# Half of batch 0's strided k moves to the software DMA queue, and every step stands in a new order

## The chip, the cores and the metric

The kernel runs on one core of a Trainium2 chip. TensorE (PE) does the matmuls, VectorE (DVE) and ScalarE (ACT) the elementwise work, GpSimd (POOL) issues most loads on a software DMA queue that converts float32 to bf16 on the way, and SyncE (SP) issues stores, transposing DMAs and plain loads on a hardware queue. The metric is device time in microseconds, lower is better; the median of the runs before is 285.81 us (three runs, 285.72 to 285.98).

## The reference

Sparse attention over 8 batches, 8 heads, 576 positions and 64 channels, followed by one dense two-layer network with the activation h·tanh(softplus(h)), which is Mish:

```python
rel = pos[:, None] - pos[None, :]
mask_local = (rel >= 0) & (rel < 32)
mask_strided = (rel >= 0) & (pos[None, :] % 32 == pos[:, None] % 32)
...
scores = np.where(masks, scale * (q @ k.T), -1e9)        # heads 0-3 local, heads 4-7 strided
attn_out = softmax(scores) @ v
x = attn_out.transpose(0, 2, 1, 3).reshape(4608, 512)
h = x @ w_in                                             # 512 -> 2048
out = (h * np.tanh(np.log1p(np.exp(h)))) @ w_out         # 2048 -> 512
```

## The kernel before

The 4608 tokens of the network are cut into nine blocks of 512 (block t is tokens 512t to 512t + 511). Both matrix products of a block are made with seven products in place of eight on 2x2 pieces, from prepared sums: `wis` and `wos` hold sums of pieces of the weights, `xs` sums of the tokens, `gs` sums of the activations. A block's first layer has four groups g of 512 hidden columns. Each group runs seven products of four 128x256 matmuls, on one of two PSUM sets: `set0` or `set1`, each one tile of two banks, with the single bank `ee0` or `ee1`. Between the products ACT copies one bank to the other, DVE adds a bank and a stored copy, and ACT takes three Mish activations into `gT`. Block 0 has its first 512 hidden columns made plainly (L684 is their Mish) and its second layer plainly too, while the sums of the weights are still being made.

Attention of batch b is worked in between. The strided heads are units of 72x72 scores, the local heads windows of 96 queries by 128 keys. q and k are transposed on PE for batches 0 to 2 (L201 strided, L207 local, copied out by ACT or DVE) and by transposing DMAs of SP for later ones. Scores go to the PSUM pair `at` or to banks of the sets, ACT takes exponentials into `Ps` and `Pl`, DVE masks them, PE multiplies by v (L306), DVE divides by the row sums (L318, L320) into `x_s` and `x_l`, and these are transposed into `xT`. `vs` is strided v spread with a column of ones from `vraw` (one step on DVE), and `vl` is local v with 32 rows copied between windows (the "share" step).

At the start nothing is in the chip. PE runs filler matmuls on `wis` (a memset tile) that nobody reads. SP's hardware queue loads batch 0's strided k as float32 into two halves, `hh[0]` and `hh[1]` (heads 4 and 5, heads 6 and 7); DVE and ACT cast one each into `ks`. POOL's software queue loads everything else.

The order is written out by hand-held strings of steps, one word each (such as `T:ks1:f@0`, the transposes of the second half of batch 0's ks into bank f). A program goes through the strings once, and every engine does its part of the words in that order and waits by semaphores where a tile is not ready. `D` and `A` at a word's end name DVE and ACT. A caret moves a word to the next block. Two words need to be known: `un` is a filler matmul, and `hold` makes POOL wait for a transposing DMA before it issues the loads behind it. Here is the part of the start that speaks of k:

```python
for hp in range(2):
    stage_ks(hp)
...
"ld:qs@0 ld:vs@0 kc:0:D kc:1:A un:1:a un:1:a ..."
```

Of the kernel before, what the change touches and what calls it, by code (L numbers as in the profile page):

```python
# [19 lines left out]
SU = 80  # L20
# [25 lines left out]
def kernel(ctx, tc, q, k, v, moe_w_in, moe_w_out, out):  # L46
# [81 lines left out]
    def load_str(b, n, src):  # L128
        if b == 0:
            Po.dma_start(raw[n][0:SU], rows80(src, 4, 4))  # L130
        else:
            Po.dma_start(raw[n][0:PN], src[b, 4:8].rearrange("h (p j) d -> p h (j d)", j=CS))

    def stage_ks(hp):
        nc.sync.dma_start(hh[hp][0:SU], rows80(k, 4 + 2 * hp, 2))

    def cast_ks(hp, eng):
        cast(eng, ks[0:SU, 2 * hp:2 * hp + 2, :], hh[hp][0:SU])
# [32 lines left out]
    def load_w_in(f0, f1):  # L171
        Po.dma_start(w_in[:, :, f0:f1], moe_w_in.rearrange("(cc p) f -> p cc f", p=128)[:, :, f0:f1])
# [382 lines left out]
    with tc.manual_schedule():  # L555
        Sc.preload_act_table(AF.Exp)
        Sc.dma_start(consts[:], consts_h.ap())
        for hp in range(2):
            stage_ks(hp)
# [48 lines left out]
        def do(w, t):  # L608
            if w[0] == "^":
                w, t = w[1:], t + 1  # L610
# [16 lines left out]
            elif f == "kc":  # L627
                cast_ks(int(x[0]), eng)
            elif f == "wi":
                load_w_in(int(x[0]), int(x[1]))  # L630
# [84 lines left out]
        def go(plan, t=0):  # L715
# [3 lines left out]
        IN = (  # L719
# [23 lines left out]
        )  # L743
        SECOND = (
# [7 lines left out]
        )  # L752
# [99 lines left out]
```

## Time and profile before

| what | value |
|---|---|
| median of three runs | 285.81 us |
| the profiled execution | 286.13 us |
| its span, first to last instruction | 284.4 us |
| PE busy | 276.1 us, 97% |
| DVE, ACT busy | 220.4 us, 193.1 us |
| granted TensorE clock | 1.00 |
| software queue, hardware queue moved | 18.62 MB, 19.14 MB |

The profile is of one execution. Busy time of PE counts a matmul from its start to its modelled end, so back-to-back matmuls overlap in it, and short waits between matmuls can stand inside busy time. The bracket behind a row of the trace is the time in which the engine was idle just before, and what ended it. A DMA's landing time runs from its issue to the moment at which a waiting engine sees it.

### The profile page before, as it was taken

How to read it: one execution, taken by the hardware profiler on the slowest of the kernel's cores; microseconds unless marked ns; L12 is line 12 of the kernel's file. 1: busy time of each engine (PE TensorE's matmuls, PEld its weight loads, DVE VectorE, ACT ScalarE, POOL GpSimd, SP SyncE). 2: the span in 40 equal slices, each digit the busy share in tenths (PEclk: the TensorE clock that was granted, in tenths of full speed). 3: DMA queues.
4: the chain of work that ended last, by engine and by line, in shares of the span. 5: the costliest groups of instructions: out<-in, count | busy, mean ns of one | idle time of the engine just before them, and what ended most of it. 6: DMA issues, size and time to landing. Idle time of an engine off the chain costs nothing.

```text
span 284.4 us, 7635 instructions
## 1 busy us (share of the span) xinstructions
PE 276.1 (97%) x3242; PEld 226.4 (80%) x3242; DVE 220.4 (77%) x376; ACT 193.1 (68%) x296; POOL 51.8 (18%) x65
## 2 busy tenths in 40 slices
PE   8889999999999999999999999999999999999994
PEld 2656845668988888988898888898888888888883
DVE  2588978899897897999798969885999656835753
ACT  2686884599867777669765986678879427525830
POOL 8423321350007005200350044002000000000000
PEclk9999999999999999999999999999999999999999
DMA  7999999999849988999799979998472030003003
GB/s 157 191 206 204 205 189 199 103 222 167 148 90 93 131 154 150 205 145 170 208 143 126 179 204 160 121 168 189 97 190 48 2 120 28 2 3 148 2 0 148
DMA packets 103826, 38.50 MB, mean 135 GB/s; under 512 B 85384, under 2 KB 99112, under 8 KB 103792
## 3 DMA queue, kind: packets, MB, share of 16 engines
q0 software_dynamic: 61296, 18.62, 66.7%
q1 hardware_dynamic: 42208, 19.14, 28.3%
q8 instruction: 25, 0.41, 0.6%
q10 hardware_dynamic: 288, 0.25, 0.4%
q14 instruction: 9, 0.07, 0.1%
HBM read 38.03 MB, written 9.44 MB: 167 GB/s over the span
## 4 chain that ended last, share of the span: by engine, by line
PE 90%; DMA 3%; ACT 3%; DVE 1%; issue 1%; POOL 0%; ACTq 0%; DVEq 0%; POOLq 0%
PE set L121 57%; PE ee L121 21%; PE at L306 5%; PE at L121 4%; DMA kl<-in_k_dram 3%; PE at L350 1%; PE ee L207 1%; PE ee L350 1%; ACT osb L110 1%; DVE ee L115 1%; PE set L306 0%; ACT kTl L110 0%; ACT gT L684 0%; ACT Ps L273 0%; DVE x_s L320 0%
## 5 line engine op out<-in xcount | busy, mean ns | idle before, releaser
L121 PEld LDWEIGHTS <-wis 128*128 128x128 bf16 x578 | 55.7, 98 | 11.6 <-issue 2.9
L121 PEld LDWEIGHTS <-gs 128*128 128x128 bf16 x512 | 48.9, 98 | 6.3
L121 PEld LDWEIGHTS <-gT 128*128 128x128 bf16 x448 | 42.1, 98 | 9.4
L121 PEld LDWEIGHTS <-w_in 128*128 128x128 bf16 x436 | 41.1, 97 | 8.1 <-issue 1.0
L121 PE MATMUL set<-xT,w_in 128*128 128x256 bf16 (+1 forms) x296 | 45.8, 278 | 0.4 <-ACT gT L684 0.2
L121 PE MATMUL set<-w_out,gT 128*128 128x256 bf16 (+1 forms) x304 | 46.2, 295 | 0.0
L448 ACT ACTIVATE gT<-set 128x1024 bf16<-128x1024 f32 x35 | 35.9, 1025 | 12.6 <-PE set L121 12.3
L121 PE MATMUL set<-xs,wis 128*128 128x256 bf16 x280 | 42.0, 272 | 0.3 <-DVE ee L115 0.2
L110 ACT COPY set<-set 128x512 f32<-128x512 f32 x37 | 21.4, 577 | 18.8 <-PE set L121 18.3
L115 DVE TENSOR_TENSOR hh<-set,hh 128x512 f32<-128x512 f32 x35 | 24.0, 686 | 7.2 <-PE set L121 6.9
L115 DVE TENSOR_TENSOR ee<-set,hh 128x512 f32<-128x512 f32 x35 | 24.4, 697 | 5.7 <-PE set L121 4.0
L121 PE MATMUL set<-wos,gs 128*128 128x256 bf16 x224 | 27.8, 273 | 0.0
L446 ACT ACTIVATE gT<-hh 128x512 bf16<-128x512 f32 x35 | 21.7, 633 | 1.8 <-DVE hh L115 1.6
L115 DVE TENSOR_TENSOR gs<-gT,gs 128x2048 bf16<-128x2048 bf16 x16 | 19.5, 1219 | 3.3 <-issue 1.0
L673 POOL COPY hold<-xT 1x2 bf16<-1x2 bf16 x6 | 2.3, 381 | 105.4 <-DMA xT<-x_l 105.4
L444 ACT ACTIVATE gT<-ee 128x512 bf16<-128x512 f32 x35 | 20.0, 596 | 2.0 <-PE ee L121 2.0
L121 PE MATMUL ee<-xs,wis 128*128 128x256 bf16 x140 | 21.0, 273 | 0.0
L121 PE MATMUL set<-xs,w_in 128*128 128x256 bf16 x140 | 21.0, 272 | 0.0
L121 PE MATMUL ee<-xT,wis 128*128 128x256 bf16 x140 | 21.0, 273 | 0.0
L115 DVE TENSOR_TENSOR gs<-gT 128x2048 bf16<-128x2048 bf16 x16 | 19.5, 1217 | 0.0
L320 DVE TENSOR_TENSOR x_s<-at,rden 72x768 bf16<-72x768 f32 (+1 forms) x22 | 18.8, 856 | 0.8
L121 PE MATMUL ee<-wos,gT 128*128 128x256 bf16 x128 | 16.1, 273 | 0.0
(135 smaller groups left out, 439.7 us busy)
## 6 DMA issues: line engine op xcount, KB each, us to landing
out_dram<-osb SPq DMA_DIRECT2D x17, 512.0 KB, 3.3
ql<-in_q_dram POOLq DMA_DIRECT2D x8, 288.0 KB, 11.9
vl<-in_v_dram POOLq DMA_DIRECT2D x8, 288.0 KB, 12.0
w_in<-in_moe_w_in_dram POOLq DMA_DIRECT2D x4, 512.0 KB, 15.0
w_out<-in_moe_w_out_dram POOLq DMA_DIRECT2D x4, 512.0 KB, 16.9
ks<-in_k_dram POOLq DMA_DIRECT2D x7, 288.0 KB, 11.2
qs<-in_q_dram POOLq DMA_DIRECT2D x7, 288.0 KB, 10.4
vraw<-in_v_dram POOLq DMA_DIRECT2D x7, 288.0 KB, 9.4
```

The costliest lines, as they stand in the source:

```text
L110: Sc.copy(out_, in_)
L115: eng.tensor_tensor(out=out_, in0=a, in1=b, op=op)
L121: PE.matmul(o, lhsT=lhsT, rhs=rhs, start=start, stop=stop, skip_group_check=True)
L207: PE.transpose(tr[64 * e:64 * e + 64, PL * j:PL * j + PL], src[0:PL, 2 * hp + e, j, :], ident[0:PL, 0:PL],)
L306: PE.matmul(po[:, (n - n0) // per, (n - n0) % per, :], lhsT=pt[0:r, c0:c0 + 128], rhs=rhs, start=True, stop=True,)
L320: Dv.tensor_tensor(out=xo, in0=po[0:m, :, :, 0:D], in1=rd.unsqueeze(3).to_broadcast([m, nb, per, D]), op=ALU.mult,)
L350: PE.transpose(tr[:, n * j:n * j + n], x[0:n, u:u + 2, :].rearrange("p u d -> p (u d)"), ident[0:n, 0:n],)
L444: Sc.activation(o[:, 0:2, 256:512], two(E), AF.Mish)
L446: Sc.activation(o[:, 2:4, 256:512], two(h[:, 1, :]), AF.Mish)
L448: Sc.activation(o[:, :, 0:256].rearrange("p (b u) n -> p b u n", b=2), SET[z][:, 0:2, :].rearrange("p b (u n) -> p b u n", u=2), AF.Mish,)
L673: Po.tensor_copy(hold[0:1, 0:2], src)
```

## The change

Of batch 0's strided k, SP loads and ACT casts only the first half (heads 4 and 5); the software queue loads the second half straight into `ks`, as its first load. The `w_in` loads can take part of the rows, and a leading underscore moves a word one block back. All strings are replaced by a list with one string for each of ten stages, so that no two blocks share one, and the order of the words is new throughout: the order was made by counting a two-bank PSUM tile as one thing that is busy or free, where a bank was counted before.

```diff
     def load_str(b, n, src):
         if b == 0:
-            Po.dma_start(raw[n][0:SU], rows80(src, 4, 4))
+            h = 2 if n == "ks" else 0
+            Po.dma_start(raw[n][0:SU, h:4], rows80(src, 4 + h, 4 - h))
...
-    def stage_ks(hp):
-        nc.sync.dma_start(hh[hp][0:SU], rows80(k, 4 + 2 * hp, 2))
-
-    def cast_ks(hp, eng):
-        cast(eng, ks[0:SU, 2 * hp:2 * hp + 2, :], hh[hp][0:SU])
+    def stage_ks():
+        nc.sync.dma_start(hh[0][0:SU], rows80(k, 4, 2))
+
+    def cast_ks(eng):
+        cast(eng, ks[0:SU, 0:2, :], hh[0][0:SU])
...
-    def load_w_in(f0, f1):
-        Po.dma_start(w_in[:, :, f0:f1], moe_w_in.rearrange("(cc p) f -> p cc f", p=128)[:, :, f0:f1])
+    def load_w_in(f0, f1, c0=0, c1=4):
+        Po.dma_start(w_in[:, c0:c1, f0:f1], moe_w_in.rearrange("(cc p) f -> p cc f", p=128)[:, c0:c1, f0:f1])
...
-        for hp in range(2):
-            stage_ks(hp)
+        stage_ks()
...
-            if w[0] == "^":
-                w, t = w[1:], t + 1
+            while w[0] in "^_":
+                w, t = w[1:], t + (1 if w[0] == "^" else -1)
...
-            "ld:qs@0 ld:vs@0 kc:0:D kc:1:A un:1:a un:1:a un:1:a un:1:a un:1:a un:1:a un:1:a un:1:a clear:1 clear:0 b:s1:C@0 "
+                "ld:ks@0 un:1:a un:1:a ld:qs@0 un:1:a un:1:a un:1:a un:1:a un:1:a un:1:a ld:kl@0 kc:A clear:1 un:1:a "
...
-        go(IN)
-        go(SECOND, 1)
...
+        for t, plan in enumerate(PLANS):
+            go(plan, t)
```

Three places show what moves. The first is POOL at the start, which issues the loads of the software queue. Before:

```order
L130 DMA qs<-in_q_dram 80x4x512
L154 DMA vraw<-in_v_dram 80x4x512
L143 DMA kl<-in_k_dram 96x4x384
L143 DMA ql<-in_q_dram 96x4x384
L159 DMA vl_78<-in_v_dram 96x24x64
L172 DMA w_in<-in_moe_w_in_dram 128x4x512 x3
L132 DMA ks<-in_k_dram 72x4x512
```

And now:

```order
L131 DMA ks<-in_k_dram 80x2x512
L131 DMA qs<-in_q_dram 80x4x512
L144 DMA kl<-in_k_dram 96x4x384
L155 DMA vraw<-in_v_dram 80x4x512
L144 DMA ql<-in_q_dram 96x4x384
L160 DMA vl_78<-in_v_dram 96x24x64
L173 DMA w_in<-in_moe_w_in_dram 128x2x512
L173 DMA w_in<-in_moe_w_in_dram 128x4x512
L173 DMA w_in<-in_moe_w_in_dram 128x2x512
L133 DMA ks<-in_k_dram 72x4x512
```

Half of ks stands ahead of everything, kl and vraw have changed places, and the first piece of w_in is cut in two with the second piece between.

The second is DVE at the start, after its memsets: the copies of transposed k and q, the spread of v and the norms of batch 0. Before (ee_103 and ee_104 are ee0 and ee1, set_101 and set_102 are set0 and set1):

```order
L112 COPY kTs<-ee_104 128x8x72
L112 COPY qTs<-ee_103 128x8x72
L112 COPY vs<-vraw 72x32x64
L112 COPY kTl<-ee_103 128x576
L318 RECIPROCAL rden<-at 72x2x4
L320 TENSOR_TENSOR x_s<-at,rden 72x512
L318 RECIPROCAL rden<-set_102 72x2x6
L320 TENSOR_TENSOR x_s<-set_102,rden 72x768
L318 RECIPROCAL rden<-set_101 72x2x6
L320 TENSOR_TENSOR x_s<-set_101,rden 72x768
L112 COPY vl_78<-vl_78 32x4x5x64
```

And now, from the spread of v on:

```order
L112 COPY vs<-vraw 72x32x64
L112 COPY kTl<-ee_104 128x576
L319 RECIPROCAL rden<-at 72x2x4
L321 TENSOR_TENSOR x_s<-at,rden 72x512
L319 RECIPROCAL rden<-set_102 72x2x6
L321 TENSOR_TENSOR x_s<-set_102,rden 72x768
L112 COPY vl_78<-vl_78 32x4x5x64
L319 RECIPROCAL rden<-set_101 72x2x6
L321 TENSOR_TENSOR x_s<-set_101,rden 72x768
```

The copy behind the spread takes the other half of kl, whose bank ee1 the first half of ql needs next, the copies of ks and qs ahead of it are one fewer, and the share of vl stands ahead of the last strided norm.

The third is ACT at the first exponentials of batch 1, behind the load of their table. Before:

```order
L675 ACT_TABLE_LOAD
L275 ACTIVATE Ps_84<-at 72x2x432
L275 ACTIVATE Ps_86<-at 72x2x288
L273 ACTIVATE Ps_85<-ee_103 72x432
L273 ACTIVATE Ps_85<-ee_104 72x432
L275 ACTIVATE Pl_88<-at 128x2x384
```

And now:

```order
L675 ACT_TABLE_LOAD
L276 ACTIVATE Ps_84<-at 72x2x432
L274 ACTIVATE Ps_85<-ee_103 72x432
L274 ACTIVATE Ps_85<-ee_104 72x432
L276 ACTIVATE Ps_86<-at 72x2x288
L276 ACTIVATE Pl_88<-at 128x2x384
```

The two exponentials from the ee banks come ahead of the second one from `at`.

More of the change, by code (lines that the diff above doesn't have):

```diff
@@ L627, in do @@
             elif f == "kc":
-                cast_ks(int(x[0]), eng)
+                cast_ks(eng)
             elif f == "wi":
-                load_w_in(int(x[0]), int(x[1]))
+                load_w_in(*(int(c) for c in x))
             elif f == "wo":
@@ L717, in go @@
                 do(w, t)
-        IN = (
[23 rows of a table removed]
-        )
-        SECOND = (
[7 rows of a table removed]
-        )
-        THIRD = (
[10 rows of a table removed]
-        )
-        MAIN = (
[8 rows of a table removed]
-        )
-        M5 = (
[8 rows of a table removed]
-        )
-        M6 = (
[7 rows of a table removed]
-        )
-        P7 = (
[5 rows of a table removed]
-        )
-        PLAIN = (
[4 rows of a table removed]
-        )
-        LAST = (
-            "m1c:D g:1 m5:0 m5:1 m5c:A g:2 m6:0 m6:1 g:3 m2:0 m6c:A m2:1 m7:0 m7:1 m7c z:b:D w:b:S m3:0 m3:1 m3c "
-            "st:1 m4:0 m4:1 z:1:A z:0:D w:0:S w:1:A "
-        )
-        go(IN)
-        go(SECOND, 1)
-        go(THIRD, 2)
-        for t in range(3, NBLK):
-            main = {5: M5, 6: M6}.get(t, MAIN)
-            if t + 1 < B:
-                go(" ".join(w for w in main.format(n1=t + 2, n2=t + 3).split() if int(w.partition("@")[2] or 0) < B), t)
-            else:
-                go(P7 if t + 1 == B else PLAIN, t)
-        go(LAST, NBLK)
+        PLANS = (
+            (
[24 rows of a table added]
+            ),
+            (
[7 rows of a table added]
+            ),
+            (
[9 rows of a table added]
+            ),
+            (
[8 rows of a table added]
+            ),
+            (
[8 rows of a table added]
+            ),
+            (
[8 rows of a table added]
+            ),
+            (
[7 rows of a table added]
+            ),
+            (
[5 rows of a table added]
+            ),
+            (
[5 rows of a table added]
+            ),
+            (
+                "g:1 g:2 m2:0 m5c:A m6:0 m6:1 m6c:A m2:1 m7:0 m7:1 g:3 m3:0 z:b:D w:b:S m3:1 m7c m3c st:1 m4:0 m4:1 "
+                "z:1:A z:0:D w:0:S w:1:A "
+            ),
+        )
+        for t, plan in enumerate(PLANS):
+            go(plan, t)
 _INS = ['q', 'k', 'v', 'moe_w_in', 'moe_w_out']
```

151 rows, old and new, of tables (IN, M5, M6, MAIN) are left out of this document.

## The prediction

> **What bounds the kernel now.** I read the page's first part, then busy time by stretches, then the first 27 us in order of time with the DMA queues beside them.
>
> ```profile
> span 284.4 us, 7635 instructions
> PE 276.1 (97%) x3242; PEld 226.4 (80%) x3242; DVE 220.4 (77%) x376; ACT 193.1 (68%) x296; POOL 51.8 (18%) x65
> ```
>
> TensorE (PE) is the bound, and the matmuls of the two programs differ by six fillers alone. So the change can gain only where PE waits. Where that is, the stretches show (first columns: stretch in us, its length, PE busy):
>
> ```profile
> 0.00:20.00 20.00, 16.89 (x248) 9.38 (x248) 10.28 (x31) 11.74 (x17) 10.79 (x18) 1.00 1.20 183
> ...
> 20.00:23.50 3.50, 3.25 (x21) 1.47 (x20) 3.43 (x11) 1.60 (x3) 1.31 (x2) 1.00 1.25 205
> 23.50:31.00 7.50, 7.16 (x79) 6.16 (x79) 6.01 (x14) 6.29 (x11) 3.63 (x5) 1.00 1.27 204
> ...
> 57.00:63.00 6.00, 5.43 (x102) 4.00 (x102) 5.94 (x12) 6.00 (x12) 3.43 (x4) 1.00 1.62 212
> ...
> 102.50:131.00 28.50, 28.50 (x359) 24.90 (x357) 24.83 (x43) 21.43 (x34) 6.24 (x7) 1.00 1.29 167
> ```
>
> The start loses most, 57 to 63 us loses 0.57 (ACT has no idle time there), and a later block loses nothing that busy time shows. The granted clock is 1.00 throughout. So the sum is made mainly of the start, and this is its supply of data, the DMA work up to 5.2 us and the landing times of what was issued by then:
>
> ```profile
> q1 hardware_dynamic: 316, 0.61, 46.4%
> ...
> issues: line engine op xcount, KB each, median us to landing
> ...
> qs<-in_q_dram POOLq DMA_DIRECT2D x1, 320.0 KB, 7.3
> vraw<-in_v_dram POOLq DMA_DIRECT2D x1, 320.0 KB, 8.2
> kl<-in_k_dram POOLq DMA_DIRECT2D x1, 288.0 KB, 8.8
> ql<-in_q_dram POOLq DMA_DIRECT2D x1, 288.0 KB, 9.3
> ```
>
> Not one packet of the software queue (q0) has moved by 5.2 us, though its first load was issued at 1.29 (below). In the next 0.8 us (5.1 to 5.9) the two queues change places, and from 5.9 to 6.7 q0 has the engines alone:
>
> ```profile
> q1 hardware_dynamic: 60, 0.10, 60.6%
> q0 software_dynamic: 62, 0.06, 47.3%
> ...
> q0 software_dynamic: 162, 0.17, 124.0%
> ```
>
> Then the rows of the start that carry the sum (start us, length us, engine, line, operation; in brackets the idle time before it and what ended it):
>
> ```profile
> 1.29 0.76 POOL L130 DMA_DIRECT2D qs<-in_q_dram  x1 [0.84 <-POOLq L836]
> 2.04 0.65 POOL L154 DMA_DIRECT2D vraw<-in_v_dram  x1
> 2.67 0.68 POOL L143 DMA_DIRECT2D kl<-in_k_dram  x1
> 3.33 0.68 POOL L143 DMA_DIRECT2D ql<-in_q_dram  x1
> ...
> 10.22 0.69 DVE L112 COPY vs<-vraw 72x2048 bf16<-72x2048 bf16 x1 [0.57 <-DMA vraw<-in_v_dram]
> 12.72 0.76 DVE L112 COPY kTl<-ee 128x576 bf16<-128x576 bf16 x1 [1.81 <-PE ee L207]
> 13.63 0.69 DVE L320 TENSOR_TENSOR x_s<-at,rden 72x512 bf16<-72x512 f32 x1
> 14.23 1.18 ACT L110 COPY qTl<-ee 128x576 bf16<-128x576 bf16 x2 [0.85 <-PE ee L207]
> 15.62 0.95 DVE L320 TENSOR_TENSOR x_s<-set,rden 72x768 bf16<-72x768 f32 x1
> 16.30 0.81 ACT L275 ACTIVATE Pl<-set 128x768 bf16<-128x768 f32 x1 [0.17 <-PE set L121]
> 16.60 0.48 DVE L112 COPY vl<-vl 32x1280 bf16<-32x1280 bf16 x1
> 17.81 0.23 DVE L318 RECIPROCAL rden<-set 96x12 f32<-96x12 f32 x1 [0.72 <-PE set L306]
> 23.48 0.60 PE L121 MATMUL set<-xT,w_in 128*128 128x256 bf16 x4 [0.25 <-ACT gT L684]
> 24.79 0.60 PE L121 MATMUL set<-xT,w_in 128*128 128x256 bf16 x4 [0.18 <-ACT set L110]
> 26.09 0.42 PE L201 MATMUL at<-consts_sb,ks 72*128 72x72 bf16 x8
> ```
>
> Issue plus landing gives the arrivals: qs 8.6, vraw 10.2, kl 11.5, ql 12.6. The reader sees a chain of arrivals, DVE and ACT behind which the first expert block (from 23.48 in its regular form) stands.
>
> **The change, part by part.**
>
> *When the software queue starts.* I take it that q0 waits for the engines until q1's backlog is through, as the two fences on it suggest. Removing one of the two hh loads then brings q0 forward by what the second one costs. Its row of landings reads, for the two,
>
> ```profile
> DMA to landing us min/median/max: 4.7/5.1/5.5
> ```
>
> issued at about 0.74 and 1.20, hence landed at 5.4 and 6.7: 1.3 us. q0 would begin at 5.2 - 1.3 = 3.9. That it can be ready so early is bounded by its fastest later start: the load of ks issued at 85.77 into an empty queue moved nothing in the window 85.7 to 87.05, and its first packets right after:
>
> ```profile
> DMA packets 0, 0.00 MB, mean 0 GB/s; under 512 B 0, under 2 KB 0, under 8 KB 0
> ...
> ks<-in_k_dram POOLq DMA_DIRECT2D x1, 288.0 KB, 5.0
> ```
>
> So it takes 1.3 us, and 1.29 + 1.3 = 2.6 is before 3.9. The other bound is no shift at all (a rival below); I take 3.9, because q0 takes over engine by engine just as q1 ends. The Trainium skill (DMA: Bandwidth & Descriptors, section "Queues, rings and completion order") speaks against this reading: each DMA engine takes turns between the queues that have work, packet by packet. The trace shows q0 silent beside 316 packets of q1; by the Trainium skill q0 would not have been ready before 5.2, and the time would be that of the first rival.
>
> *What each load then does.* Half of ks is 160 rows, at 162 rows per 0.8 us another 0.8 us of q0. The new issue order is ks half, qs, kl, vraw, ql, vl. ks half: 8.6 - 1.3 - 0.8 (half as many rows as qs) = 6.5; qs: 8.6 - 1.3 + 0.8 = 8.1; kl no longer behind vraw (10.2 - 8.6 = 1.6): 11.5 - 0.5 - 1.6 = 9.4; vraw behind kl (11.5 - 10.2 = 1.3, my estimate 1.4 with rounding): 10.2 - 0.5 + 1.4 = 11.1; ql 12.6 - 0.5 = 12.1. All later loads come 0.5 us sooner; in the old order PE had no wait for a load after 20 us, and the moves of q and k of batch 1 and 2 among them are of one load's length (1.5 us, as from vraw to kl). I cost them at nothing; the cover is the time between landing and use (by my count of the work ahead, 1 us or more), and if it goes, PE waits for the difference.
>
> *The attention of batch 0.* DVE now spreads v before it copies kl's first half, so both stand behind vraw: 11.1 + 0.69 = 11.8, + 0.76 = 12.6. Then the norms, each with a reciprocal of about 0.22: 0.91 to 13.5, 1.17 to 14.7, the share of vl 0.48 to 15.2, 1.17 to 16.4. Before, the same work ended at 17.08. But the next norm waits for ACT: it idled 0.72 until 17.81. ACT's path: ql's first half is transposed when the bank of kl's copy is free (12.6 to 13.0), the second after the norm at 13.5 (13.8 to 14.1), its copy of 0.6 to 14.75, then two exponentials of 0.8 to 16.4 (before 16.30 + 0.81 = 17.1), the products with v, and the norm at 16.95 in place of 17.81. That is -0.85, inside DVE's own -0.7 (16.4 against 17.08 plus idle time). Norms, transposes and the first products of the expert layer follow as before: **-0.85**.
>
> *PE's wait for the first Mish.* The transposes of batch 1's ks (26.09) now stand ahead of the product at 23.48, in the 0.25 us in which PE idles: **-0.25**. The other half's transposes stand where PE idled 0.18 for ACT (24.79): **-0.2**.
>
> *Six more fillers.* Before the first real transpose stand 17 of 0.2 to 0.43 us on an idle PE; they end at about 6.5, when ks half lands: 0, and 0.4 if it lands sooner. The cast that leaves DVE (1.01 us) and the one that stays on ACT (1.04) lie beside them: 0.
>
> *Exponentials of batch 1.* These rows set the pace at 37 to 41 us:
>
> ```profile
> 37.05 1.28 ACT L675 ACT_TABLE_LOAD   x1
> 38.47 0.89 ACT L275 ACTIVATE Ps<-at 72x864 bf16<-72x864 f32 x1
> 39.87 0.65 ACT L275 ACTIVATE Ps<-at 72x576 bf16<-72x576 f32 x1 [0.52 <-PE at L121]
> 40.41 0.93 ACT L273 ACTIVATE Ps<-ee 72x432 bf16<-72x432 f32 x2
> ```
>
> The 0.93 now comes ahead of the 0.65, and the next scores need the bank that the 0.65 frees. ACT idled 0.52 there, which hides that much; bounds 0 and +0.93, taken 0.93 - 0.52, rounded down for q·k that are issued earlier: **+0.3**.
>
> *57 to 63 us.* The same ACT work in another order, ACT without idle time: 0, with ±0.4 from a single exponential. Two of the three sums of w_out leave DVE's queue ahead of the copies of ql, the share of batch 2's vl comes in ahead of them; 0 while vl has landed.
>
> *Blocks from 63 us and the tail.* Small moves of steps, transposing DMAs of batch 3 some blocks' steps earlier on SP, holds and loads on POOL moved with them. PE had no idle time there; 0, bounds -0.57 and +0.57 (what the stretch of 57 to 63 us, the nearest with such moves, has of idle PE). The last steps of the program are the same.
>
> Sum: -0.85 - 0.25 - 0.2 + 0.3 = -1.0. The profiled execution took 286.13 us (span 284.4, 1.7 around it); it would be 285.1. The median of the runs shown is 0.32 below that execution, so I predict **284.8 us**.
>
> **The rivals.**
>
> *The software queue has its own start* (slower). If q0 begins at 5.2 whatever q1 holds, the ks half costs 0.8 and nothing is given back: vraw lands at 10.2 + 0.8 + 1.4 = 12.4, DVE's chain ends at 17.7 in place of 17.08, and with kl's copy at 13.9 the first ql transposes, ACT's copies and exponentials follow by 1.3 us against my forecast: the norm at 18.35, +0.55. With -0.25 and +0.3 as above that is +0.6: 286.4. It decides once vraw lands later than 12.0. For it: no packet of q0 for 3.9 us after the issue. Against: q0 takes over just when q1's packets run out, and needed 1.3 us at 85.77. I give 0.2. By the Trainium skill's rule of taking turns (same page and section) it would be the likely case.
>
> *The lead is used up at 50 to 60 us* (no change). DVE has the share of vl of batch 2 ahead of the copies of kl and ql now:
>
> ```profile
> vl<-in_v_dram POOLq DMA_DIRECT2D x1, 288.0 KB, 12.3
> ...
> 60.17 0.48 DVE L112 COPY vl<-vl 32x1280 bf16<-32x1280 bf16 x1
> ```
>
> Issued at 42.85, it landed at 55.2, five us before its old use; the new use is near 54.5. One load less ahead of it (1.5) and the 0.5 make 53.2; a DMA that is 1.3 later than this would hold DVE, and with ACT full, PE: about 1 us, 285.8. Chance 0.17.
>
> *The order does more than its rows show.* Counting a two-bank tile as one in the order could remove waits that I left alone: the 0.34 us of PE idle from 23.5 to 31 and the 0.57 from 57 to 63. Then 284.8 - 0.9 = 283.9, and 283.3 with the -0.57 of the later blocks. Chance 0.1.
>
> **How the numbers follow.** My forecast has 0.53, around 284.8 with its own range 284.0 to 285.5 (0.4 from 57 to 63, 0.57 from the later blocks, not both at once); the rivals 0.2, 0.17 and 0.1. The range that holds 8 in 10 goes from the third rival's 283.3 to the first one's 286.4 plus 0.4: 283.3 to 286.8. A measurement tells about 0.2% (0.57 us) from no change. Faster: 0.53 and 0.1 less a small part near the edge: 0.61. Same: the second rival and that part: 0.18. Slower: the first rival and a hundredth: 0.21.
>
> **What the changed profile would show.** Right: q0's first packets near 3.9 us; spread of v at about 11.1; the norm of the first local heads at about 17.0; the first product of the regular expert form at 22.4 to 22.7; PE idle from 57 to 63 still about 0.6. Wrong: q0 still silent until 5.2 with v's spread past 12; DVE waiting for vl near 54; PE waiting for DMA-transposed k or q after 63; or a lead at 23 us that is gone at 63.

## The result, and the profile after

The changed kernel is slower: a median of 297.47 us (296.48 to 302.09, four executions) against 285.89 us beside it, a ratio of 1.0394 (1.0348 to 1.0441). Here and below a median is over all executions of a kernel, a ratio over those within 1.5% of its shortest. The profiled execution is the longest of the four, 302.09 us, with a start that a second profile of the same kernel does not have, so the readings below are set against that one (after_again). This is the page after, its busy time, granted clock and the chain that ended last:

```profile
span 300.3 us, 7647 instructions
PE 283.0 (94%) x3242; PEld 231.7 (77%) x3248; DVE 218.5 (73%) x373; ACT 196.7 (66%) x298; POOL 52.3 (17%) x67
...
PEclk9977999999999999899999999997799999999999
...
PE 78%; DMA 11%; DVE 4%; ACT 2%; issue 1%; POOL 1%; SPq 0%; DVEq 0%; POOLq 0%
```

PE is idle for 17 us of the span (8 before), 11% of the last chain are DMAs (3% before), and the clock, which was whole from one end to the other, falls at three places (digits under 9). Four of the stretches that the prediction used, and two later ones (stretch, length, busy PE, PE loads, DVE, ACT, POOL, granted clock, DMA share, GB/s):

```profile
0.00:20.00 20.00, 16.53 (x223) 9.37 (x224) 7.43 (x27) 10.54 (x15) 10.54 (x18) 0.98 1.19 176
20.00:23.50 3.50, 2.99 (x30) 2.22 (x31) 2.14 (x5) 2.46 (x3) 1.40 (x2) 0.50 1.24 206
23.50:31.00 7.50, 7.48 (x58) 4.75 (x57) 4.57 (x12) 3.80 (x7) 2.26 (x4) 0.84 1.27 203
57.00:63.00 6.00, 5.60 (x109) 3.52 (x107) 5.90 (x10) 5.17 (x8) 2.60 (x3) 1.00 1.03 142
...
116.00:128.00 12.00, 7.23 (x77) 5.62 (x76) 6.47 (x12) 3.38 (x6) 0.47 (x1) 0.87 2.97 127
190.00:214.00 24.00, 20.58 (x222) 17.11 (x220) 15.78 (x26) 14.75 (x22) 0.17 (x1) 0.86 0.95 138
```

The start and two places in the later blocks lost time; from 23.5 to 31 PE is busy all the time, at a lower clock. The start first, the software queue between 3.4 and 5.2 us and then DVE (the bracket is the idle time before a row and what ended it):

```profile
q0 software_dynamic: 258, 0.25, 94.8%
```

```profile
11.59 0.69 DVE L112 COPY vs<-vraw 72x2048 bf16<-72x2048 bf16 x1 [2.17 <-DMA vraw<-in_v_dram]
17.61 0.48 DVE L112 COPY vl<-vl 32x1280 bf16<-32x1280 bf16 x1 [2.33 <-DMA vl<-in_v_dram]
19.15 0.22 DVE L319 RECIPROCAL rden<-set 96x12 f32<-96x12 f32 x1
```

The software queue starts 1.7 us sooner, where 1.3 were predicted (before, no packet of it moved up to 5.2). Yet DVE stands 2.33 us for vl, and the norm of the local heads is at 19.15, not 16.95.

The first later place is block 3. SP's transposing DMAs of batch 3's output (xT; by tile, shortest, median and longest ns, first and last start), then in order of time these, the first of POOL's five loads of batch 5 beside them, and who waits:

```profile
L328 SPq DMA_TRANSPOSE xT<-x_l x2: 1227/1706/2184, 109.8 to 112.1; - x2
```

```profile
109.82 3.51 SPq L328 DMA_TRANSPOSE xT<-x_l  x2
111.16 0.70 POOL L133 DMA_DIRECT2D qs<-in_q_dram  x1 [11.60 <-DMA qTs<-qs]
...
121.73 0.43 DVE L115 TENSOR_TENSOR xs<-xT,xs 128x512 bf16<-128x512 bf16 x1 [5.37 <-DMA xT<-x_l]
...
124.80 3.46 PE L121 MATMUL set<-w_out,gs 128*128 128x256 bf16 x16 [4.77 <-DVE osb L115]
```

The second of the two, issued at 112.1, is waited for until 121.73, 9.6 us. DVE does its steps in the order of the program, so all its other work stands behind that sum, and PE behind DVE. The old order had a hold on POOL near this point (the `hold` copy, which waits for xT), the new one has it a block later. But this hold of the old order stood behind four loads, and here that order shows more than a hold:

```profile
106.48 3.16 SPq L327 DMA_TRANSPOSE xT<-x_l  x2
...
109.44 0.72 POOL L132 DMA_DIRECT2D qs<-in_q_dram  x1 [18.42 <-DMA qTs<-qs]
```

The second of these two was issued at 108.4 and the first load 1.0 us behind it; the two landed in 3.0 and 5.0 us. In the new order the first load, at 111.16, is 0.9 us ahead of the second.

The second place is the head of block 6, with batch 7's transposing DMAs, in order of time:

```profile
185.50 3.49 SPq L188 DMA_TRANSPOSE kTl<-kl  x1
189.09 6.34 SPq L188 DMA_TRANSPOSE qTs<-qs  x1
...
203.23 1.31 SPq L188 DMA_TRANSPOSE qTl<-ql  x1
...
207.65 0.50 PE L121 MATMUL at<-qTl,kTl 64*128 64x96 bf16 x8 [3.42 <-DMA qTl<-ql]
...
209.36 1.34 DVE L112 COPY xT<-ks 128x576 bf16<-128x576 bf16 x2 [6.38 <-DMA ks<-x_s]
```

The kernel before issued the first two of these in 1.3 and 1.6 us, at a time (183 to 191 us) in which the software queue moved 0.04 MB, where it moved 1.20 MB in the changed kernel. They landed in 3.8 and 4.1 us there, in 11.6 and 10.5 here:

```profile
185.48 1.34 SPq L187 DMA_TRANSPOSE kTl<-kl  x1
...
188.76 1.61 SPq L187 DMA_TRANSPOSE qTs<-qs  x1
```

### The profile page after: what moved, and what is told of

Read it like the earlier page. It is cut to its first block, busy times and chain, and to the rows that moved or that the text cites. A ratio compares the mean times of both kernels' runs of the same rounds, so it can differ in the third digit from the quotient of the medians.

```text
span 300.3 us, 7647 instructions
## 1 busy us (share of the span) xinstructions
PE 283.0 (94%) x3242; PEld 231.7 (77%) x3248; DVE 218.5 (73%) x373; ACT 196.7 (66%) x298; POOL 52.3 (17%) x67
## 4 chain that ended last, share of the span: by engine, by line
PE 78%; DMA 11%; DVE 4%; ACT 2%; issue 1%; POOL 1%; SPq 0%; DVEq 0%; POOLq 0%
PE set L121 51%; PE ee L121 17%; DMA vl<-in_v_dram 4%; PE at L307 4%; DMA qTl<-ql 4%; PE at L121 4%; DMA xT<-x_l 3%; DVE gs L115 2%; PE ee L351 1%; PE at L351 1%; ACT gT L445 0%; PE ee L208 0%; PE set L351 0%; ACT gT L447 0%; PE at L202 0%
## 5 line engine op out<-in xcount | busy, mean ns | idle before, releaser
L121 PEld LDWEIGHTS <-wis 128*128 128x128 bf16 x584 | 56.8, 99 | 12.1 <-issue 2.9
L121 PEld LDWEIGHTS <-gs 128*128 128x128 bf16 x512 | 50.8, 101 | 12.6 <-DVE gs L115 3.6
L121 PE MATMUL set<-xT,w_in 128*128 128x256 bf16 (+1 forms) x295 | 47.5, 284 | 0.3 <-issue 0.2
L449 ACT ACTIVATE gT<-set 128x1024 bf16<-128x1024 f32 x35 | 35.9, 1025 | 10.8 <-PE set L121 8.2
L121 PE MATMUL set<-wos,gs 128*128 128x256 bf16 x224 | 29.2, 283 | 0.0
L110 ACT COPY set<-set 128x512 f32<-128x512 f32 x31 | 17.9, 578 | 12.8 <-PE set L121 12.7
L110 ACT COPY osb<-set 128x1024 f32<-128x1024 f32 x9 | 9.1, 1013 | 21.1 <-PE set L121 20.5
L121 PE MATMUL set<-w_out,gs 128*128 128x256 bf16 x112 | 15.4, 292 | 4.8 <-DVE osb L115 4.8
```

Of the source, the lines that this page charges most:

```text
L110: Sc.copy(out_, in_)
L121: PE.matmul(o, lhsT=lhsT, rhs=rhs, start=start, stop=stop, skip_group_check=True)
L449: Sc.activation(o[:, :, 0:256].rearrange("p (b u) n -> p b u n", b=2), SET[z][:, 0:2, :].rearrange("p b (u n) -> p b u n", u=2), AF.Mish,)
```

## The experiments

The theory after the profile (A): transposing DMAs of SP share the DMA engines with the loads of the software queue; the new order lets loads run beside them and asks for some late, and what waits for them stops DVE or PE for 3 to 6 us, with half clock behind it. Rivals were the split of k, SP's own queue, and the new plans' order on the engines. One table for the main profiles: the time in us at which the last norm of a batch begins, and the span. The last column is the median over the timed executions.

| kernel | batch 1 | batch 3 | batch 4 | batch 6 | batch 7 | span | median |
|---|---|---|---|---|---|---|---|
| before | 50.4 | 102.4 | 129.0 | 188.3 | 216.5 | 284.4 | 285.9 |
| after, first profile | 54.4 | 106.0 | 139.1 | 199.9 | 232.5 | 300.3 | 297.5 |
| after_again | 50.8 | 102.1 | 137.5 | 198.3 | 229.8 | 297.5 | 299.1 |
| no_loads567 | 49.1 | 101.3 | 127.8 | 188.6 | 214.9 | 282.7 | 285.7 |
| split_alone | 50.3 | 102.1 | 128.9 | 188.2 | 216.4 | 284.3 | 285.6 |
| no_split | 49.2 | 101.7 | 135.6 | 196.4 | 226.6 | 294.3 | 298.4 |
| start_only | 49.6 | 102.6 | 129.2 | 188.5 | 216.7 | 284.6 | 286.4 |
| first_three_b | 49.4 | 101.0 | 128.0 | 187.3 | 215.5 | 283.4 | 286.8 |
| hold3 | 49.8 | 101.6 | 128.4 | 190.4 | 221.3 | 289.1 | 290.6 |
| last_six | 49.9 | 101.9 | 128.8 | 191.7 | 221.8 | 289.5 | 290.6 |
| no_holds | 49.9 | 105.5 | 132.1 | 191.4 | 219.6 | 287.4 | 289.2 |
| hold3_ql | 49.5 | 107.0 | 133.5 | 198.6 | 228.6 | 296.3 | 295.8 |
| hold3_sp | 50.0 | 101.7 | 128.2 | 189.9 | 219.2 | 287.0 | 290.9 |
| hold3_order | 49.4 | 103.1 | 130.1 | 194.4 | 227.2 | 294.9 | 293.9 |

**after_again.** Nothing is changed.

> The changed kernel, nothing altered. In its first profile the share of v waited 2.3 us for vl, which landed at 17.6 us, and the clock fell to half from 19 to 26. Theory A': that belongs to that one execution: vl lands near 15, the last norm of batch 0's local heads is at 18.5 us or before, the clock stays whole in the start, and the two stalls with half clock behind them (near 116 and 200 us) stand: 296 to 298.5. Rival E, it is the rule for this order: vl lands at 17 or later again and the half clock in the start is there.

299.07 us, ratio 1.0457 (1.0407 to 1.0507). The clock is whole in the start, and both stalls stand:

```profile
16.70 0.48 DVE L112 COPY vl<-vl 32x1280 bf16<-32x1280 bf16 x1 [1.38 <-DMA vl<-in_v_dram]
18.23 0.22 DVE L319 RECIPROCAL rden<-set 96x12 f32<-96x12 f32 x1
...
121.97 0.80 PE L121 MATMUL set<-w_out,gs 128*128 128x256 bf16 x3 [5.87 <-DVE osb L115]
...
206.07 0.35 PE L121 MATMUL at<-qTl,kTl 64*128 64x96 bf16 x8 [3.47 <-DMA qTl<-ql]
```

So the half clock from 19 to 26 is not the rule for this order (of the later profiles only that of hold3_b has it at this place, for 3.5 us). The wait for vl is smaller, not absent: between both theories' numbers.

**split_alone, no_split, start_only.** The first puts the split into the kernel before:

```diff
-            Po.dma_start(raw[n][0:SU], rows80(src, 4, 4))
+            h = 2 if n == "ks" else 0
+            Po.dma_start(raw[n][0:SU, h:4], rows80(src, 4 + h, 4 - h))
...
-            "ld:qs@0 ld:vs@0 kc:0:D kc:1:A un:1:a
+            "ld:ks@0 ld:qs@0 ld:vs@0 kc:0:D un:1:a
```

> The kernel before with nothing but the split of batch 0's strided k. Theory A, the new order delays the share of v (where the loads stand, and nothing to fill PE): vl lands by 15.3 us, half a microsecond behind before's 14.8, and the time is 285.3 to 286.4. Rival B, the split itself does it (the software queue carries 0.33 MB more ahead of vl, and its engines run unevenly): vl lands near 17.6 here too, PE waits some 2.8 us more for it in the start, and the time is 288 to 290. Under both the software queue's first packet comes near 3.5 us in place of 5.2.

The second takes it out of the changed kernel:

```diff
-                "ld:ks@0 un:1:a un:1:a ld:qs@0 ... ld:kl@0 kc:A
+                "un:1:a un:1:a ld:qs@0 ... ld:kl@0 kc:0:A kc:1:D
```

> The changed kernel with strided k by the sync queue in both halves again, all else in the new order. Theory A (order): the start still loses 3 to 5 us, and the time stays at 296 to 298. Rival B (split): vl lands near 15, the half clock between 19 and 26 us is gone, and the time falls by 3 to 5 us, to 292.5 to 294.5. The stalls at 120 and 204 us stay under both.

The third has the new plan of the start and the old ones behind it, without the steps that the new plan already holds:

```diff
+        PLANS = (<new plan 0>, <SECOND without x:0 x:1 x:2 so:1 so:2 sh:D ld:vl@3>, <THIRD>, <MAIN> ...)
```

> The new plan for the start (with the split), then the old plans for all later blocks. Theory A: the losses add, so the start's 4.6 us remain and both later stalls (4.9 us at 120, 3.4 at 204) with their half clock go: 289.5 to 291.5. Rival C, the later stalls come from the start's delay, which shifts the blocks against the transfers, and not from where the later plans put loads and transposing DMAs: a stall of 3 us or more near 120 or 204 is seen here too, and the time is 294 to 298.

The split alone gives 285.64 us, ratio 0.9983 (0.9967 to 0.9999); without it the changed kernel takes 298.39, ratio 1.0464 (1.0402 to 1.0525); the new start alone 286.40, ratio 1.0018 (1.0003 to 1.0032). Neither the split nor the start makes the loss, and rivals B and C are out. Theory A had the start of no_split lose 3 to 5 us; it lost nothing (batch 1's last norm at 49.2, 50.4 before), so its time came out near the range without that part of the reason. My 289.5 to 291.5 for the new start was wrong, since it counted the first profile's 4.6 us there as the rule.

**no_loads567.** The eighteen loads of batches 5 to 7 are left out; every other step stays.

```diff
-... ld:ks@5 3:2 Z:2 st:0 7:3 H:2 3:3 ld:qs@5 X:0:a@3 ...
+... 3:2 Z:2 st:0 7:3 H:2 3:3 X:0:a@3 ...
```

> The changed kernel without the eighteen loads of batches 5, 6 and 7 (its later batches work on what the tiles hold; all transposing DMAs, holds and steps stay in place). Theory A, the stalls come from loads beside and ahead of the transposing DMAs: none of over 1 us is left on PE after 80 us, the clock stays whole, 284.5 to 286.5 us. Rival J, the plans of blocks 3 to 6 stall by their own order on the engines and the sync queue, whatever the loads do: waits of 2 us or more at 116 to 122 and at 198 to 206 us, 291 or above.

285.65 us, ratio 1.0007 (0.9981 to 1.0033); the profiled execution took 284.46. The same stretches as above:

```profile
116.00:128.00 12.00, 12.00 (x143) 10.69 (x141) 10.89 (x20) 6.76 (x10) 0.17 (x1) 1.00 0.57 136
190.00:214.00 24.00, 24.00 (x295) 20.90 (x294) 20.98 (x35) 18.78 (x28) 0.17 (x1) 1.00 0.18 51
```

PE has no gap in either, and the clock is whole. With all steps, holds and transposing DMAs where the new order puts them, the stalls need the loads: rival J is out. Batch 7's local k and strided q, 3.5 and 6.3 us on SP above, go through in 1.4 and 1.6:

```profile
166.99 1.44 SPq L188 DMA_TRANSPOSE kTl<-kl  x1
...
170.18 1.60 SPq L188 DMA_TRANSPOSE qTs<-qs  x1
```

Against this kernel, after_again falls behind by 1.7 us up to batch 1's last norm (0.8 at batch 3's), 8.9 more up to batch 4's (9.7 - 0.8), none up to batch 6's (9.7), and 5.2 more up to batch 7's (14.9). Its span is 14.8 longer, so 14.1 of 14.8 us are lost at two places.

**hold3.** The hold on batch 3's output stands right behind its second transposing DMA, two loads of batch 5 behind the hold.

```diff
-... 7:3 H:2 3:3 ld:qs@5 X:0:a@3 ...
+... 7:3 H:2 3:3 X:0:a@3 ...
-sp:D ld:vl@5 m1:1 g:2 _y:1@3 m5:0 ...
+sp:D m1:1 g:2 _y:1@3 hold@3 ld:qs@5 ld:vl@5 m5:0 ...
-... m6c:D __hold@3 g:3 ...
+... m6c:D g:3 ...
```

> The changed kernel with the hold on batch 3's transposed local output brought up right behind its second transposing DMA, and the loads of batch 5's strided q and local v put behind the hold. Theory A, loads of the software queue that run beside the transposing DMA make it slow: both land within 5 us of their issue, the 4.8 us stall of PE at 120 us and the half clock to 128.4 are gone, and the time falls by 4 to 6.5 us, to 291 to 293.5. Rival D, the sync queue itself is late (a transposing DMA and two stores stand ahead): they land 9 us after issue as before, and the time stays within 1.5 us of 297.5.

290.63 us, ratio 1.0163 (1.0126 to 1.0199), 6.8 us less than the changed kernel and 0.4 below theory A's range. SP's rows, by tile and in order of time, are the same as in the stall, only the loads come later, the first at 113.3:

```profile
L328 SPq DMA_TRANSPOSE xT<-x_l x2: 1215/1660/2106, 105.7 to 107.9; - x2
```

```profile
105.72 3.42 SPq L328 DMA_TRANSPOSE xT<-x_l  x2
...
112.73 0.43 DVE L115 TENSOR_TENSOR xs<-xT,xs 128x512 bf16<-128x512 bf16 x1 [0.77 <-DMA xT<-x_l]
112.76 0.44 POOL L673 COPY hold<-xT 1x2 bf16<-1x2 bf16 x1 [17.58 <-DMA xT<-x_l]
```

The second DMA, issued at 107.9, is there at 112.7: 4.8 us in place of 9.6, after the same stores and the same transposing DMA ahead of it. Rival D is out for this place.

**no_holds.** The mirror image in the kernel before, without its five holds, of which the diff shows one.

```diff
-... v:l0:A@3 hold@2 ld:ks@4 ...
+... v:l0:A@3 ld:ks@4 ...
```

> The kernel before without its five holds: no load waits any more for the transposing DMAs of the local output. Theory A, loads that run beside transposing DMAs make them late: those of the local output land in 6 to 10 us in place of 3 to 5, one or more waits of over 2 us for a transposed tensor stand on PE after 80 us, with half clock behind them, and the time is 288 to 296. Rival D, the lateness came from the sync queue alone: the waits stay under 1 us each, and the time is within 1 us of 285.9.

289.16 us, ratio 1.0119 (1.0079 to 1.0160), with one large stall, at batch 2's output. Without the holds, and then the kernel before at the same place:

```profile
79.70 0.70 POOL L132 DMA_DIRECT2D ks<-in_k_dram  x1 [18.31 <-DMA kTs<-ks]
...
80.55 2.55 SPq L327 DMA_TRANSPOSE xT<-x_l  x2
...
91.30 0.61 PE L121 MATMUL set<-xT,w_in 128*128 128x256 bf16 x4 [2.57 <-DMA xT<-x_l]
91.37 0.42 DVE L115 TENSOR_TENSOR xs<-xT,xs 128x512 bf16<-128x512 bf16 x1 [3.49 <-DMA xT<-x_l]
```

```profile
81.05 2.52 SPq L327 DMA_TRANSPOSE xT<-x_l  x2
...
84.93 0.63 POOL L673 COPY hold<-xT 1x2 bf16<-1x2 bf16 x1 [23.04 <-DMA xT<-x_l]
85.77 0.70 POOL L132 DMA_DIRECT2D ks<-in_k_dram  x1 [0.21 <-issue]
```

With the hold both DMAs were through 3.9 us after the first one's issue; beside the loads, 10.8. So the old order needs this hold. The other four could go without a loss in this profile: the kernel is 3.1 us behind at batch 3's last norm and 3.1 at batch 7's. At the outputs of batches 3 to 5 most of POOL's loads waited for the transposing DMA of strided q to free their first tile, so the two of the output still came first (for batch 3 at 103.6 and 105.3, the load at 106.8) and landed in 2.4 to 4.3 us. I had expected half clock behind the wait; the clock stayed whole.

**last_six, first_three, first_three_b.** The old plans up to block 3 with the new ones from block 4, and the reverse with the new plans up to block 2.

```diff
+        PLANS = (<IN>, <SECOND>, <THIRD>, <MAIN of block 3>, <new plan 4 less the steps done>, <new plans 5 to 9>)
```

> The old plans up to and with block 3, the new ones from block 4 on, in the old start. Theory A: no stall near 116 to 122 us, but the one at the head of block 6, near 198 us, with its half clock: 285.9 + 2.9 + 1.7 = 290.5, between 289 and 292.5. Rival C, that stall needs the earlier blocks' shift: 285.5 to 287.5.

```diff
+        PLANS = (<new plans 0 to 2, ld:qs@5 taken out>, <MAIN of block 3, ahead of it: m1:1 y:1@3 hold@3 ld:ql@5 ld:kl@5 ld:qs@5>, <old plans from block 4 on>)
```

> The new start and the new plans of blocks 1 and 2 (batch 5's strided q behind the hold), and the old plans from block 3 on. Theory A: PE's lead at 65 us (0 to 1.1 us in the runs so far) is kept, none of the two stalls is there, and the clock stays whole: 284.7 to 286.2 us. Rival I, the new plans carry a loss of their own into any later order: 287 or above.

> The new plans of the start and blocks 1 and 2 and the old ones from block 3 on, joined so that the last activation of block 2 comes ahead of the load of the other table (in the first such kernel PE waited 3.0 us for it at 111 us). Theory A: that wait goes and nothing else changes: 289.8 - 3.2 = 286.6, between 285.5 and 287.3; a lead at 65 us that is used up by 90 us, where the sums of x waited 2.3 us for batch 2's local output, speaks for no gain. Rival I: 288.5 or above.

last_six: 290.59 us, ratio 1.0158 (1.0118 to 1.0198), with PE's wait for local q at the head of block 6 (2.1 us) and half clock behind it, as theory A had it; a further wait of 1.8 us near 179 neither theory named. first_three gave 289.77, ratio 1.0140 (1.0118 to 1.0163), but 3.0 us of that are PE waiting at 111 us for an activation that my joint put behind the load of another table, which says nothing on the plans. With the joint mended (the word `_Z:3`, the last activation of block 2, put first) it is 286.83, ratio 1.0042 (1.0006 to 1.0079), from 285.15 to 290.91. The profiled execution of 285.15 has PE's lead of 1.0 to 1.4 us over the kernel before from batch 1 to batch 7 (table); no other execution has a profile, and not every one keeps the lead.

**hold3_ql, hold3_sp, hold3_qs, hold3_order, hold3_old4.** Five tries at the second stall on top of hold3.

```diff
-... 7:1 3:1 y:0 ... ^m1:0 D:ql@7 7c:3 ...
+... 7:1 3:1 D:ql@7 y:0 ... ^m1:0 7c:3 ...
```

> The kernel with the hold moved, and batch 7's transposing DMA of local q issued ahead of batch 6's first local transposing DMA, ahead of two stores, of strided k and of batch 6's second one, in place of behind them. Theory A, PE waits there only because this transposing DMA stands last in the sync queue: the 2.9 us wait near 198 us and the half clock of 3.4 us behind it (worth 1.7) go: 290.6 - 4.6 = 286 us, between 285.5 and 288, the upper end if VectorE's wait for the strided output (5.3 us there) now shows on PE. Rival F, the loads themselves are late: the wait stays within 1 us of 2.9, and the time at 290 or above.

hold3_sp adds to this the strided output (V) ahead of y:1 and its copies (vc) behind g:2:

```diff
-... H:2 y:1 Z:2 ... E:3 V _hold ...
+... H:2 Z:2 ... E:3 V y:1 _hold ...
-m1c:D m5:0 m5:1 vc:0:D@6 ae ... q:l1:F vc:1:D@6 m2:1 ... g:2 e:s0:F ...
+m1c:D m5:0 m5:1 ae ... q:l1:F m2:1 ... g:2 vc:0:D@6 vc:1:D@6 e:s0:F ...
```

> As the kernel with local q ahead, and further batch 6's strided output asked for ahead of its second local transposing DMA, and VectorE's two copies of it put behind the spread of v and the second sum of g. Theory A: VectorE no longer stands 5 us in front of these copies, and what remains of the wait on PE goes too: 285 to 286.2 us, at the kernel before or up to 0.3% below it. Rival: nothing more than the local q gives, or a copy that now comes late for the block's sums of x: 286.5 or above.

hold3_qs moves strided q of batch 6 from block 5 to block 4, and hold3_order puts batch 7's in another order:

```diff
-m1c:A ae g:1 _D:qs@6 _ld:qs@7 ...
+m1c:A ae g:1 _ld:qs@7 ...
-... D:kl@6 r:l1:A ...
+... D:kl@6 D:qs@6 r:l1:A ...
```

> The kernel with the hold moved, and batch 6's transposing DMA of strided q issued in the middle of block 4, right behind that of local k, in place of the head of block 5. The load of batch 7's strided q, first of six loads in its queue, waits for it (until 166.0 us there, 6.1 us after its issue at 159.9). Theory A, the wait near 198 us is the end of this chain (strided q of batch 6, loads of batch 7, their transposing DMAs): the loads of batch 7 start 3 to 7 us sooner, the wait and its half clock go, 285.5 to 287.5. Rival F, those DMAs are late for the traffic beside them whenever they start: the wait stays at 2 us or more, 289.5 or above.

```diff
-... D:kl@7 e:s2:F ... D:qs@7 _ld:ql@7 ... 4:2 D:ks@7 ... y:1 ... D:ql@7 ... V _hold ...
+... D:kl@7 D:ks@7 e:s2:F ... _ld:ql@7 D:ql@7 D:qs@7 ... 4:2 ... V y:1 _hold ...
```

> The kernel with the hold moved, and the transposing DMAs of batch 7 in another order on the sync queue: local k, strided k, local q, strided q, then the first of the local output, two stores, the strided output, the second of the local output. The loads stay as they are. Theory A2, what counts is the order in this queue: strided k comes some 10 us sooner, so its tile is free when the strided output is ready, local q too, both waits (PE 2.9 us near 198, VectorE 5 us behind it) go with the half clock: 285.5 to 287.5 us. Rival F, the loads beside them set the pace: a wait of 2 us or more stays between 195 and 212 us, 288.5 or above.

hold3_old4 has the old plans from block 4 on behind hold3's first four:

```diff
+        PLANS = (<hold3's plans 0 to 3>, <MAIN of block 4, ahead of it: _H:3 D:qs@5 hold@4 ld:qs@6 ld:ql@6 ld:ks@6>, <old plans from block 5 on>)
```

> The new plans up to block 3 with the hold moved, the old ones from block 4 on. Under both theories on the second stall it has no place here: 290.6 - 4.7 = 285.9, between 285.2 and 287.5. Rival I, the new plans of the first four blocks leave the transfers late for whatever follows: a wait of over 2 us on PE after 130 us, 288 or above.

None reached theory A's time; the rivals' came. hold3_ql took 295.83 us (ratio 1.0257, 1.0176 to 1.0337): the wait for local q is gone, and PE waits 2.8 us for DVE at 210, which waits 5.6 us for the strided output. Its profiled execution, the longest of four, also has waits of 2.7 us for w_out at 53.9 and of 2.7 us for strided q at 147, in steps that the edit did not touch. hold3_sp took 290.9 (1.0120, 1.0080 to 1.0160; 287.62 to 295.74): that wait of PE is gone, and one of 1.8 us for the sums of x comes at 204. hold3_qs took 297.06 (1.0289, 1.0229 to 1.0350), with waits of 1.9, 3.2 and 3.3 us on PE; POOL's load of batch 7's strided k now waits 10.3 us. hold3_order took 293.9 (1.0257, 1.0194 to 1.0321):

```profile
183.92 5.86 SPq L188 DMA_TRANSPOSE kTs<-ks  x1
...
204.40 1.34 DVE L112 COPY xT<-ks 128x576 bf16<-128x576 bf16 x2 [6.86 <-DMA ks<-x_s]
207.52 1.41 PEld L121 LDWEIGHTS <-gs 128*128 128x128 bf16 x8 [4.40 <-DVE gs L115]
```

Strided k, now second, held SP for 5.9 us (2.6 in hold3), and strided q, now fourth, for 2.8 (4.2 in hold3): the one that is issued while the loads run pays, as rival F said. hold3_old4 (old plans from block 4 on) took 298.26 and tells nothing: my joint put two stores behind a transposing DMA that waited for its load until 155, and ACT waited 8.3 us for their buffer.

**hold3_fill, and hold3_b beside hold3_fill_b.** Twelve products that nobody reads fill PE's wait at 198.

```diff
-... m2:0 q:l0:A sh:A ...
+... m2:0 un:12:a q:l0:A sh:A ...
```

> The kernel with the hold moved, and twelve 512-column products that nobody reads on PE just ahead of the first product of batch 7's local scores, where PE waits 2.9 us. They take some 2.6 us of that wait and shorten nothing. Theory G, the half clock follows from PE being idle for about 3 us, and costs 1.7 us by itself: the clock stays whole near 198 us and the time falls to 288.3 to 289.8. Rival H, the half clock has another cause, or the products hold up what follows: 290.3 or above.

> The kernel with the hold moved once more, beside the next: 289.5 to 291.7 us again, one wait of about 3 us on PE near 198 us and 3.4 us of half clock.

> The same with the twelve unread products in that wait. Theory G, 3.4 us of half clock cost 1.7 us: 1.2 to 1.7 us below the kernel beside it, with the clock whole. Rival H: within 0.7 us of it, or slower.

hold3_fill took 289.70 us, ratio 1.0108 (1.0050 to 1.0165). From 190 to 214 us, hold3 and then hold3_fill:

```profile
190.00:214.00 24.00, 21.13 (x238) 17.68 (x237) 16.81 (x29) 14.98 (x23) 0.18 (x1) 0.93 0.33 55
```

```profile
190.00:214.00 24.00, 23.43 (x260) 19.16 (x259) 17.73 (x31) 16.11 (x25) 0.18 (x1) 1.00 0.39 79
```

The fillers kept the clock. What that is worth the pair did not settle: side by side on one chip hold3_b took 284.52, 289.77, 295.89 and 298.68 us and hold3_fill_b 289.41 to 292.50. The price can be read inside hold3: from batch 6's last norm to batch 7's first it needs 20.6 us, the kernel without the loads 16.0, and of the 4.6 between them 2.9 are the wait for local q. The 1.7 left match half of the 3.4 us of half clock behind it.

```profile
190.42 0.19 DVE L319 RECIPROCAL rden<-at 72x8 f32<-72x8 f32 x1
...
211.00 0.23 DVE L319 RECIPROCAL rden<-at 96x12 f32<-96x12 f32 x1 [0.48 <-PE at L307]
```

```profile
188.56 0.19 DVE L319 RECIPROCAL rden<-at 72x8 f32<-72x8 f32 x1
204.58 0.23 DVE L319 RECIPROCAL rden<-at 96x12 f32<-96x12 f32 x1 [0.48 <-PE at L307]
```

No kernel here beats the kernel before by more than the split alone does, 0.2% with an interval that ends at 0.9999.

## Why the prediction was wrong

*When the software queue starts: right.* First packets at 3.5 us against a forecast of 3.9; without the split (no_split) they come between 4.5 and 5.0. The split also halves the queue's first load, and no run separates this from the lighter other queue. The Trainium skill (DMA: Bandwidth & Descriptors, section "Queues, rings and completion order") has each DMA engine take turns between the queues that have work. From this the prediction drew that the start would stay at 5.2; here it did not.

*What each load then does: right on average, too narrow.* vraw landed at 10.8 to 11.6 us (forecast 11.1). vl was where it went wrong: I gave it no landing time, although the share of vl was moved ahead of a norm. DVE waited 2.3 us for it in the first profile, 1.4 in the second, 0 to 0.5 in hold3 and first_three_b.

*The attention of batch 0 and the small gains: right where vl came in time.* The norm that was to be at 16.95 instead of 17.81 stood at 17.05 in first_three_b, 16.97 in no_loads567, 17.3 in no_split and start_only, 17.6 in hold3, 18.2 and 19.15 in the two profiles of the changed kernel. Where no load was late the new order had its forecast lead over the kernel before: by the table 1.3 us at batch 1's last norm without the late loads, and at batch 3's 0.3 in after_again, 0.8 in hold3, 1.4 in first_three_b. The first product of the regular form, forecast at 22.4 to 22.7, stood at 22.7 to 23.1 in no_loads567, first_three_b, no_split and start_only, so part of the lead came later than its rows said. Nor does the lead need the software queue's early start, on which the forecast of the norm was built: at batch 1's last norm no_split has it (49.2 for 50.4), split_alone has not (50.3). Single executions came near the forecast of 284.8 (284.46 in no_loads567, whose median is 285.65, and 284.52 in hold3_b, whose others take 289.8 to 298.7); that is luck as much as confirmation.

*Six fillers, exponentials, 57 to 63 us:* PE's idle time from 57 to 63 was 0.40 us in the first profile and 0.62 in the second (0.57 before), inside the bounds; the lead at batch 1 does not speak for more than the +0.3.

*Blocks from 63 us: this step failed.* I wrote that small moves of steps, "transposing DMAs of batch 3 some blocks' steps earlier on SP, holds and loads on POOL moved with them" cost 0, bounds -0.57 and +0.57, since "PE had no idle time there". The two stalls cost 8.9 and 5.2 us in the second profile. That PE had no idle time shows that nothing was late in the old order, and not how much later it could be. What covered these blocks was that the transposing DMAs came ahead of the loads, by a hold or by POOL's wait for a free tile: from 80 us on, the trace of before has none that was issued less than 8 us behind a load. The prediction listed holds, loads and transposing DMAs as moved, and put no price on a load that comes first. The row for it was there: at block 3 xT landed in 3.0 and 5.0 us with the loads behind it. No row showed it with loads ahead, and there it took 9.6. So the upper bound of 0.57 was not a bound.

*The rivals.* That the software queue has its own start did not happen. That DVE waits for vl near 54 did not happen either; it waited for the earlier vl, of batch 0. Near 54 PE waited 2.1 to 2.7 us for w_out instead, in the profiles of hold3_ql, hold3_fill_b and hold3_old4. Of the signs of being wrong, the one that came is PE and DVE waiting for DMA-transposed tensors after 63 us. No rival had it as a mechanism.

What stays open is the second stall. It needs the loads (no_loads567) and comes with the new plans from block 4 on alone (last_six). Which of these steps would have to go back was not found, and no run tells how much of it comes from loads running beside the transposing DMAs and how much from their own data coming late. At both places the runs show that loads that come first make these DMAs late; that this is by sharing the DMA engines stays theory A's reading.

## What to carry to other kernels

A wait that keeps an engine from issuing transfers can be what makes other transfers quick: before a hold is moved or dropped, list what runs in its shadow and who waits for that, and price both. "The bound engine has no idle time there" covers a move only as far as the slack of each transfer that it shifts, which is the time from its landing to its use and has to be read for each of them. At the first stall the repair was to put the loads behind the transposing DMAs again. At the second, bringing one late transfer forward only made another one late, and no repair was found.

## What the runs showed of the hardware

- A transposing DMA beside loads of the software queue is slower in two ways: it lands in 9.6 us where the same one lands in 4.8 (hold3), and its issue holds SP for 3.5 and 6.3 us (local k and strided q of batch 7) where the same two take 1.4 and 1.6 without the loads (no_loads567). The Trainium skill (DMA: Bandwidth & Descriptors, section "Rules for kernel authors") says that a transpose next to ordinary DMAs needs nothing. It says so beside a rule on corrupted data; in time these runs show the cost above.
- The granted clock fell to half behind short waits, and not behind every one. In hold3_qs a wait of 1.9 us on PE was enough, first the wait and then the clock behind it:

```profile
144.68 0.19 PE L121 MATMUL set<-qTs,kTs 64*128 64x72 bf16 x1 [1.91 <-DMA qTs<-qs]
```

```profile
145.10:148.50 3.40, 3.40 (x22) 2.25 (x16) 1.95 (x4) 2.23 (x4) 3.35 (x5) 0.50 0.86 208
```

  In first_three a wait of 3.03 us left it whole:

```profile
111.03 0.39 PE L121 MATMUL set<-w_out,gT 128*128 128x256 bf16 x2 [3.03 <-ACT gT L449]
```

```profile
111.00:116.00 5.00, 4.97 (x71) 4.06 (x72) 1.11 (x2) 4.49 (x7) 2.61 (x3) 1.00 0.26 42
```

  The Trainium skill (TensorE: Matmul & The Clock Gate, Part 1) has the clock at half after an idle window of about 3.4 us. The length of the low stretches, 3.4 to 3.5 or 6.8 to 6.9 us, agrees with such a window. That a wait of 1.9 us was enough does not agree.
- One kernel's executions can lie far apart: hold3_b from 284.5 to 298.7 us, while the kernel before stayed within 285.4 and 286.8 beside it. That transfers without slack are the reason is my reading; no run shows it.
